# Batch 0's state softmax from scores with tokens as rows, and a new order for the first sixth of the steps

## The chip, the core and the metric

The kernel runs on one core of a Trainium2 chip. The metric is the device time of one execution, in microseconds, as the median of the runs.

## What is computed

```python
scores = scale * np.matmul(x, state.transpose(0, 1, 3, 2))     # x [8,8,512,64], state [8,8,32,64]
a = softmax over the 32 states (exp of scores minus their maximum, over sum + 1e-9)
xread = np.matmul(a, state)                                    # 512 rows per batch and head
scores2 = scale * np.matmul(state, x.transpose(0, 1, 3, 2))
a2 = softmax over the 512 tokens
sread = np.matmul(a2, x)                                       # 32 rows per batch and head
x = concat([xread, sread], axis=2), heads side by side: [4352, 512]
h = x @ w_in                                                   # w_in [512, 2048]
g = softplus(h)
out = g @ w_out                                                # w_out [2048, 512]
```

The weights of the MLP come as 64-bit numbers and are put together as fp32 on the chip.

## The kernel before

The eight heads of a batch go in two groups by the parity of the head (e = 0, 1); four heads of 32 states fill the 128 rows of a tile. For the token rows the first GEMM is not made from xread: the states times W ("V", `v_product`) are made first and then multiplied with the softmax weights (`gemm1`). TensorE makes the scores with states as rows and tokens as columns (`scores`, step Q); both softmaxes start from the same scores. The softmax over the tokens (steps e, f, i, t, u, R) runs along a row. The softmax over the states runs across rows: `a_turn` (step 1) turns blocks of 32 by 32 on VectorE so that the states of a token lie beside each other, `a_max`, `a_sub`, `a_exp`, `a_sum`, `a_mul` (2 to 6) work on groups of 32, and `a_back` (7) turns the result back on VectorE. For batch 0 the steps 1 to 7 go by halves of 256 tokens (two keys, (0, 0) and (0, 1)), both head groups in one tile; `span` gives the half. For the other batches a key is a head group.

W is loaded in ten pieces (step I) and each is put together in three steps: `win_upper` (a, ScalarE), `win_lower` (b, ScalarE or VectorE), `win_join` (c, VectorE). W_out (O) goes the same way by A, B, C and is then split into two fp32r parts, `wout_hi` (D) and `wout_lo` (E). Batch 0 goes through GEMM 1 (g), softplus (s) and GEMM 2 (G) directly; its first four column blocks of GEMM 1 and first two of GEMM 2 are full fp32, the rest three fp32r passes. The other batches use sums of blocks and products of their own (steps F, H, L, M and others), which the change does not touch.

The order is fixed: a string, `PLAN`, has one character for each step, and the kernel emits the steps in that order; each engine runs its own instructions in program order. SyncE issues all DMAs. A second table, `ENG`, names for some steps the engine that each occurrence runs on (D VectorE, A ScalarE, P GpSimd). Tiles live in "rooms": `take` gives out the tag that has been free longest, `done` counts down its uses. There are eight PSUM banks (`banks`).

```python
    for k in PLAN:
        now[0] = k
        count[k] = count.get(k, 0) + 1
        next(run[k])
```

All instructions are recorded with the line of one helper (L100), so the rows below are told apart by tile and shape: W, ST (the states), ident (transposes on TensorE), d, s, g, v (rooms in SBUF), b (PSUM banks).

Of the kernel before, what the change touches and what calls it, by code (L numbers as in the profile page):

```python
# [15 lines left out]
ALU = mybir.AluOpType  # L16
AX = mybir.AxisListType
PSUM = bass.MemoryType.PSUM

P = 128  # L20
B, H, S, NS, D = 8, 8, 512, 32, 64
# [8 lines left out]
F1, F2 = 4, 2  # L30
# [7 lines left out]
FORMS = (1, 2, 6, 5, 7, 3, 4)  # L38
SLAB = {5: 0, 6: 1, 7: 2, 4: 3, 1: 4, 2: 5, 3: 6}
PLAN = (  # L40
    "TSTSIITITIQI1IQ2O3e12e34dfbaafb4c565OOIIOc6vttQvahb7huecabfuhhbac78gtvggghe1cbhgguaA8c98BC89gvgshsGhll99DUGssB"
    "Am1EWCDbEn2fAaBmcnCgGggGGGGGgbABasmssDCcnEm3XjIXOOIKjvRGGnDsam4mAhhliAlBnBbcnCrYCbEGGggGgGGgGsaDDs2c3mmssEnjSj"
    "jjjjSjKjjjOjTTjOJvvGhhhll5m4hUnEGGgGgn5llU66WAsmdBmsGQvGnYChDlhnE7l7ei89eGggGGsWmsBA8Y9nmn1CUGgGGgKjjjKjKTKTjj"
    "jDffssmEWnY21U32gGGGtttWsouuuoQvvh1lefUYWhUGgshoggKjKKpjKJJjKXglUelogggssWsfsss4Fh3lYHWYggggKXKgsssssHHF5FLYLL"
    "MgRyMMKKppKJJpJJsFFzHkHLFH2LFLrZHkHH4HMMML5L66LkLkk7i1kHMJXXJJMRvvykr8Fh73q9l2h8H9qlkhh4HlMMJPXJJTJlzZkkk35Lgg"
    "gggsLkssss4vvMMgh5qkhlkHhdhsqLLqlllgMgggggMsssssFq67HkLJJJPJPPPXggggMssssHF8LHsHFM6LF7FHFLLkkHMMJJJPJHHkkqqkLL"
    "q98MMtytvuhzHkkuLHlFFLZLhvRMMJJPJJMMHl9kHkhHLHhkLgMMlkirqkLqLklkkPTJJPPJJPJJXXvQvgse1fhshhlq1ell2qh3qggggsssfs"
    "4ggMgggsH2l53LgMg4ssssssgggssHs5Fk6ki7LFHFFHLFHFLtytMMMMkLH6uzkuLZqkHvvRJJJJPTMMhhLlHH7hlHh8q98FLLllkkrMMJJJTJ"
    "XPLFqHLqkk9HLMMgggMMsHsskkqkkkLkJPPJJPTJJXPvQv1khhql2qlee13ggggssshsHfhf42llLgggMgggsHFqL35sss4ssgggMsssH56F6k"
    "LFHkLFH7MMttyF8HqFLu7L9kuzHkLFMJPJPJJMMMJJPPJPPRvHZkkHFqLiLkHh8vMMkLlrHhHhHqLlLlkkH9LLqMJXPTJPPJJJJMgMggMssshk"  # L50
    "kHkklkkvvQge1hfsgggshsshH2Lll3h1l2leLFgggg4sssfsggggssssgMMM3FHFqsH4F5FqqLH5Lqk6LTPPJJJPMtytMMJJXJHFFHkLiuk7kH"
    "HHHzL6HLqLZkukLMMkFMvvRJJPh8hH7kLqlq9LrqLh8MMMJTJPXJJJPPXJPl9kHkhkkklgMMskklkvQvgghqHl1ehe2sfhfLlh13lqgggssss4"
    "Lq253qgggwiMyPssgHs45MgJzlsgFPLstkuJgkxsgssgtgsMH6sqL7H86PuMFZRLvvkrFJkhlvhlPvhhFFJHFLhlh97MHLlHHMHLMwFkMkHJJ8"
    "hLJJJlPq9MHgLkxsgkgMFsslPwgHgLJqPkLghkMqMgxkHsskgPkskgLJgJgsllqsPLMHLHyzMqZsPwssMkgggqLggskg&P&wsxsxMgkqwkx%%s"
    "wgswx&xqP&%s%s&g%w&wP%wJsxxgwJxxw&x%&%sF&gFw&wx%&%qxg%wHx&s&Lg%H%&sL%&&%s%sHLHLMFHMHFPFJFHHkJFLFLFLLFJkHMLMFJk"
    "JHLHFkkJMHHLHkLqMHkPLHkFLLJLJHMHLqLJHFkMHPFqkLJLHHkHPFLHMMLJkLMHLHkkkkLJMLqMkPkkHHqPqkqLkqLqPPqMPMkPqMPkqkPP"
)
ENG = {
    '&': "DDAADDADDDDADADA",
    '3': "PPDDDPPDPDDPDDDP",  # L60
    '6': "PPDPPPPDDPDDDPPP",
    '8': "PPDPAPDPDPPDAADPDD",
    '9': "DPDPDDDPPDPDDPDDPP",
    'B': "DAAADDAA",
    'D': "PDPAAADA",
    'E': "DDDPDPPD",
    'F': "DPDDDDDDPDPDPDDPDDPDPDDPDDPDPPDPPDPDPDDDPDPPDPPDDPDDDDPDDDDDDPDD",
    'H': "PAAAAPAAAADPAADAPAAAAAAPADPPAAPDDPPDAAPAADDAPDAADADDPAADAAAPAPAPAAPADAAAPAPAAAAPADADAADAAAAAAAAPAAAAPAAADAAAAPAA",
    'L': "DDDDDDDDPDPDPPPDDDDPPDDDPDPPPDPDDDPDDPPPPPDDPDDDPDDPDPDDDPDDDPDDDPDDDDPDPDPDDPPDPPPPPPDDDDDDDDDDPDPDPDDDPDDDDPDD",
    'U': "PPDDDPDP",  # L70
    'W': "AAADAPAD",
    'Y': "DDDPPPDD",
    'b': "AAAAADDDDD",
    'h': "AAAADADDDDDDDADAADADDDAADDAAADADAADDAADADAAAADAAAAADADADADADDAAAAAAA",
    'k': "AADDDDDDDDDDDDDDAADDDDDDDDDDDDDDAADDDDDDDDDDDDDDAADDDDDDDDDDDDDDDDDDDDDDDDDDDDDDAADDDDDDDDDDDDDDAADDDDDDDDDDDDDDDDDDDDDD",
    'm': "DAADAADAAAPADP",
    'n': "DDDPDDDPPDPDDD",
    'o': "AAAD",
    'q': "PPDPDPDDPDPDDPDPPPDDDDPPPPPPPDDPDDPPDDDPPPDDPDDDDPPPDPDPDDDD",
    'u': "DAADDAADDADADDDD",  # L80
    'w': "PADDADAAAAAAAAAA",
    'x': "DDPPPPDPDDDDDPDP",
    'z': "DDADAADA",
# [51 lines left out]
def attention_then_softplus_mlp(ctx: ExitStack, tc, xn, xt, zq, zp, stk, w_in, w_out, out):  # L135
    nc = Ordered(tc) if PIN else tc.nc
# [13 lines left out]
    r2 = Rooms(sp, "s", N2, [P, 512])  # L150
    r4 = Rooms(sp, "d", N4, [P, 2, 512])
    banks = Rooms(ps, "b", 8, [P, 512])
    r1 = Rooms(sp, "v", N1, [P, P])
# [4 lines left out]
    ident = cp.tile([P, P], F32, name="ident")  # L158
    make_identity(tc.nc, ident)
    ST = cp.tile([P, B, 4, 2 * NS], F32, name="ST")  # L160
# [6 lines left out]
    def engine():  # L167

        k = now[0]
        i = count[k] - 1  # L170
        return ENG[k][i]

    def cast(dst, src, e):
        if e == "A":
            nc.scalar.copy(dst, src)
        elif e == "D":
            nc.vector.tensor_copy(dst, src)
        else:
            nc.gpsimd.tensor_scalar(dst, src, 1.0, 0.0, ALU.mult, ALU.add)

    def elementwise(dst, a, b, op, e):
        (nc.vector if e == "D" else nc.gpsimd).tensor_tensor(dst, a, b, op)
# [3 lines left out]
    xT, x, win, wraw = {}, {}, {}, {}  # L186
# [16 lines left out]
    def load_xT():  # L203
        for b, i in HALVES:
            if b == 0:
                t = xT[b, i] = r4.take([P, 4, S // 2])
                nc.sync.dma_start(t.t, xt[b, :, :, S // 2 * i:S // 2 * i + S // 2])
            else:
                t = xT[b, i] = r4.take()
                nc.sync.dma_start(t.t, xt[b, :, 2 * i:2 * i + 2, :])  # L210
            yield
# [123 lines left out]
    def units(b):  # L335
        return UNITS.get(b, UNIT)
# [3 lines left out]
    for b, f0, f1 in TURNS + [(b, 0, NFT) for b in range(2, B)]:  # L340
        for ft in range(f0, f1):
            i = next(i for i, (c0, c1) in enumerate(units(b)) if c0 <= P * ft < c1)
# [4 lines left out]
    def heads(out_e, b, rhs):  # L347
        for q in range(4):
            for e in range(2):
                r = slice(64 * e, 64 * e + 64)  # L350
                nc.tensor.matmul(out_e[e][32 * q:32 * q + 32], ST[r, b, q, 32 * e:32 * e + 32], rhs(q)[r], start=True, stop=True,
                                 tile_position=(64 * e, 32 * q))
# [37 lines left out]
    sc, T, e2, a2, pr, sr, aT = {}, {}, {}, {}, {}, {}, {}  # L390
# [6 lines left out]
    def span(b, u):  # L397
        return slice(S // 2 * u, S // 2 * u + S // 2) if b == 0 else slice(0, S)


    few = {}

    def mx(b, i):
        return few[b][:, 16 * i:16 * i + 16]
# [10 lines left out]
    def scores():  # L415
        for b in range(B):
            for u in range(2 if b == 0 else 1):
                n = S // 2 if b == 0 else S
                if u == 0:
                    sc[b, 0], sc[b, 1] = [banks.take(uses=4 if b == 0 else 3) for _ in range(2)]  # L420
                    few[b] = r1.take(uses=3)
                heads([sc[b, e][:, n * u:n * u + n] for e in range(2)], b, lambda q: xT[b, u][:, q] if b == 0 else xT[b, q // 2][:, q % 2])
                xT[b, u].done()
                if b:
                    xT[b, 1].done()
                yield

    def spread(t):
        return t.unsqueeze(2).broadcast_to([P, 16, NS])

    def flat(t):
        return t.rearrange("p a n -> p (a n)")

    def a_turn():
        for b, i in KEYS:
            t = T[b, i] = r2.take([P, 16, NS])
            if b == 0:
                for e in range(2):
                    nc.vector.transpose(flat(t[:, 8 * e:8 * e + 8]), sc[b, e][:, span(0, i)])
                    sc[b, e].done()  # L440
            else:
                nc.vector.transpose(flat(t.t), sc[b, i].t)
                sc[b, i].done()
            yield

    def a_max():
        for k in KEYS:
            nc.vector.tensor_reduce(mx(*k), T[k].t, AX.X, ALU.min if k[0] else ALU.max)
            yield

    def a_sub():
        for k in KEYS:
            elementwise(T[k].t, T[k].t, spread(mx(*k)), ALU.subtract, engine())
            yield

    def a_exp():
# [19 lines left out]
    af = {}  # L476

    def a_back():
        for k in KEYS:
            af[k] = r2.take(uses=4 + F1 if k[0] == 0 else 2)  # L480
            nc.vector.transpose(af[k].t, flat(T[k].t))
            T[k].done()
            yield

    def part(b, i, e):
# [462 lines left out]
    def fold_store():  # L948
# [13 lines left out]

    steps = {
        "S": load_state, "d": scale_state, "T": load_xT, "X": load_x, "I": load_win, "O": load_wout,
        "a": win_upper, "b": win_lower, "c": win_join,
        "A": wout_upper, "B": wout_lower, "C": wout_join, "D": wout_hi, "E": wout_lo,
        "v": v_product, "h": v_hi, "l": v_lo,
        "Q": scores, "1": a_turn, "2": a_max, "3": a_sub, "4": a_exp, "5": a_sum, "6": a_mul, "7": a_back,
        "8": a_hi, "9": a_lo, "e": s_max, "f": s_exp, "i": s_sum, "t": s_turn, "u": s_copy, "R": s_read,
        "r": s_scale, "y": s_back, "z": s_hi, "Z": s_lo,  # L970
        "w": w_hi, "x": w_lo, "g": gemm1, "&": h_copy, "%": h_add, "s": softplus, "m": g_hi, "n": g_lo, "G": gemm2,
# [67 lines left out]
```

## Time and profile before

| what | value |
|---|---|
| time, median of 3 runs | 615.14 us (614.76 to 615.14) |
| profiled execution, time | 614.1 us |
| its span | 612.3 us |
| TensorE matmul busy | 597.5 us (98%), 4048 passes |
| weight loads busy | 485.0 us |
| VectorE busy | 477.1 us (78%) |
| ScalarE busy | 306.9 us (50%) |
| GpSimd busy | 303.9 us (50%) |
| DMA | 161.62 MB, mean 264 GB/s |

The span is the part of the execution that the trace covers; 1.8 us of the profiled execution lie outside it. A busy time is the sum of the instructions' durations without their overlap. Matmul rows are pipelined, with modelled ends: the distance from one start to the next tells more of their price than their duration. An fp32 matmul is recorded as two passes, a transpose as one.

### The profile page before, as it was taken

To read this page: it belongs to the slowest core of one execution; us is meant where nothing else is said; L and a number is where in the kernel's file an instruction comes from. 1 tells how busy PE (TensorE), PEld (TensorE's weight loads), DVE (VectorE), ACT (ScalarE), POOL (GpSimd) and SP (SyncE) were. 2 spreads that over 40 slices of the span, in tenths; PEclk is the share of its full clock that TensorE was granted. 3 is DMA by queue.
4 is the path that set the end of the run, shared out by engine and by line. 5 is a ranking of instruction groups with operands and counts; after the bars stand their busy time and mean duration, and the time that the engine had idled before them with its cause. 6 is when DMAs were issued, how large, how long until landed. Compare 5 with 4: busy or idle time off the path is not lost.

```text
span 612.3 us, 10423 instructions
## 1 busy us (share of the span) xinstructions
PE 597.5 (98%) x4048; PEld 485.0 (79%) x4048; DVE 477.1 (78%) x644; ACT 306.9 (50%) x445; POOL 303.9 (50%) x190
## 2 busy tenths in 40 slices
PE   3999999999999999999999999999999999999997
PEld 1568677888788888878788787888787888888886
DVE  4999998799636896798479966699747944389996
ACT  4999767962526218631283318802675232274321
POOL 2422637517563761777276532672085955251561
PEclk9999999999999999999999999999999999999999
DMA  8999959999637888089917992699543851166572
GB/s 310 408 391 364 351 198 343 365 403 414 247 140 276 310 324 336 1 318 394 341 65 258 344 316 123 208 390 411 206 152 147 337 203 70 29 243 233 210 300 77
DMA packets 50415, 161.62 MB, mean 264 GB/s; under 512 B 4288, under 2 KB 29376, under 8 KB 37824
## 3 DMA queue, kind: packets, MB, share of 16 engines
q1 hardware_dynamic: 50368, 160.97, 70.5%
q8 instruction: 32, 0.52, 0.3%
q14 instruction: 15, 0.12, 0.1%
HBM read 137.36 MB, written 23.59 MB: 263 GB/s over the span
## 4 chain that ended last, share of the span: by engine, by line
PE 97%; DVE 1%; ACT 1%; DMA 1%; issue 0%; POOL 0%; SPq 0%
PE b L100 97%; ACT s L100 1%; DMA ST<-in_zp_dram 1%; DVE v L100 0%; DVE s L100 0%; POOL s L100 0%; SPq L100 0%; DVE W L100 0%; ACT ST L100 0%
## 5 line engine op out<-in xcount | busy, mean ns | idle before, releaser
L100 PE MATMUL b<-g,d 128*128 128x256 f32 (+1 forms) x1576 | 290.3, 337 | 0.0
L100 PEld LDWEIGHTS b<-g,d 128*128 128x128 f32 x1576 | 246.6, 190 | 36.1 <-issue 1.7
L100 PE MATMUL b<-d,d 128*128 128x512 f32 x744 | 177.2, 392 | 0.0
L100 PEld LDWEIGHTS b<-d,d 128*128 128x128 f32 x744 | 137.8, 188 | 32.3 <-issue 3.0
L100 ACT ACTIVATE g<-b 128x512 f32<-128x512 f32 x112 | 63.6, 600 | 98.7 <-PE b L100 98.3
L100 POOL TENSOR_TENSOR d<-g,d 128x1024 fp32r<-128x1024 f32 x31 | 78.6, 2538 | 53.0 <-ACT d L100 26.6
L100 DVE TENSOR_TENSOR s<-s,b 128x512 f32<-128x512 f32 (+1 forms) x105 | 68.7, 675 | 40.3 <-PE b L100 32.6
L100 DVE TENSOR_TENSOR d<-g,d 128x1024 fp32r<-128x1024 f32 x53 | 80.0, 1516 | 1.7 <-ACT d L100 1.5
L100 PE MATMUL b<-g,s 128*128 128x512 f32 (+1 forms) x280 | 71.4, 372 | 0.0
L100 ACT CAST d<-g 128x1024 fp32r<-128x1024 f32 x50 | 51.7, 1051 | 29.7 <-POOL g L100 15.8
L100 ACT ACT_TABLE_LOAD x48 | 61.6, 1283 | 1.5 <-PEq L1020 0.7
L100 PEld LDWEIGHTS b<-g,s 128*128 128x128 f32 x280 | 50.2, 188 | 12.0 <-issue 2.2
L100 ACT CAST d<-b 128x512 fp32r<-128x512 f32 x35 | 20.1, 586 | 59.3 <-PE b L100 59.3
L100 DVE TENSOR_TENSOR d<-b,d 128x512 fp32r<-128x512 f32 x62 | 41.4, 681 | 9.3 <-ACT d L100 9.0
L100 POOL TENSOR_SCALAR d<-g 128x1024 fp32r<-128x1024 f32 x20 | 29.5, 1476 | 36.2 <-DVE g L100 26.5
L100 POOL TENSOR_TENSOR s<-s,v 128x512 f32<-128x512 f32 x17 | 21.0, 1237 | 44.5 <-DVE v L100 43.9
L100 POOL TENSOR_TENSOR s<-s 128x256 f32<-128x256 f32 x29 | 29.9, 1032 | 21.1 <-DVE s L100 21.1
L100 POOL TENSOR_TENSOR d<-d,d 128x256 f32<-128x256 f32 (+2 forms) x17 | 28.3, 1664 | 18.6 <-DVE d L100 8.5
L100 PE MATMUL b<-W,ST 64*32 64x512 f32 (+2 forms) x544 | 32.6, 574 | 4.1 <-DVE W L100 4.1
L100 DVE TENSOR_REDUCE v<-s 128x16 f32<-128x512 f32 x32 | 21.6, 680 | 18.6 <-ACT s L100 18.5
L100 POOL TENSOR_TENSOR g<-g,g 128x1024 f32<-128x1024 f32 x11 | 29.4, 2671 | 11.2 <-DVE d L100 6.3
L100 ACT COPY s<-b 128x512 f32<-128x512 f32 (+2 forms) x32 | 15.2, 501 | 29.1 <-PE b L100 25.1
(82 smaller groups left out, 626.9 us busy)
## 6 DMA issues: line engine op xcount, KB each, us to landing
g<-slabs SPq DMA_DIRECT2D x98, 1024.0 KB, 6.6
d<-in_xt_dram SPq DMA_DIRECT2D x16, 512.0 KB, 7.4
g<-in_w_out_dram SPq DMA_DIRECT2D x8, 1024.0 KB, 12.5
d<-in_xn_dram SPq DMA_DIRECT2D x16, 512.0 KB, 7.6
slabs<-d SPq DMA_DIRECT2D x16, 512.0 KB, 6.9
out_dram<-s SPq DMA_DIRECT2D x56, 128.0 KB, 5.3
g<-in_w_in_dram SPq DMA_DIRECT2D x6, 1024.0 KB, 13.0
slabs<-g SPq DMA_DIRECT2D x24, 256.0 KB, 7.1
```

Source lines behind the costliest of these rows:

```text
L100: return lambda *a, **k: self.tc.keep_in_program_order(f(*a, **k))
```

## The change

Batch 0's softmax over the states no longer starts from the shared scores. `a_turn` has TensorE multiply again, with 128 tokens of x as weights and 64 state columns streaming, so that tokens come out as rows, into a PSUM bank of their own (`turned`). `a_max` and `a_sub` read that bank, both on VectorE; `a_sub` writes the SBUF tile. `a_back` is four transposes on TensorE into a bank (`back`) for each half, and a new step 0, `a_copy`, brings that bank to SBUF on ScalarE. The score banks of batch 0 have two uses instead of four, and its x tiles two instead of one. The other batches keep VectorE's transposes.

The first 278 of the 1758 characters of `PLAN` are replaced by 280: the same steps, each as often as before, and the two new ones, in another order. The engine entries of the occurrences in this stretch change too (those of 3, 6, 8, 9, B, D, E, U, b, h, m, n, u).

```diff
-    "TSTSIITITIQI1IQ2O3e12e34dfbaafb4c565OOIIOc6vttQvahb7huecabfuhhbac78gtvggghe1cbhgguaA8c98BC89gvgshsGhll99DUGssB"
...
+    "TSTSIITTQ1a2db1b3QI23ecfeac45f4vba56thIQvh6701Itc7haIbgc8he0auvggh1bufbgh8OggaAO9Osg8geIscXsBIcs9CvtGmh89f9DUl"
...
+    '0': "AA",
...
-    'D': "PDPAAADA",
...
+    'D': "DPAPDADA",
...
-                t = xT[b, i] = r4.take([P, 4, S // 2])
+                t = xT[b, i] = r4.take([P, 4, S // 2], uses=2)
...
-                    sc[b, 0], sc[b, 1] = [banks.take(uses=4 if b == 0 else 3) for _ in range(2)]
-                    few[b] = r1.take(uses=3)
+                    sc[b, 0], sc[b, 1] = [banks.take(uses=2 if b == 0 else 3) for _ in range(2)]
+                    few[b] = few.get(b) or r1.take(uses=3)
...
+    turned, back = {}, {}
+
     def a_turn():
         for b, i in KEYS:
-            t = T[b, i] = r2.take([P, 16, NS])
             if b == 0:
-                for e in range(2):
-                    nc.vector.transpose(flat(t[:, 8 * e:8 * e + 8]), sc[b, e][:, span(0, i)])
-                    sc[b, e].done()
+                few[b] = few.get(b) or r1.take(uses=3)
+                t = turned[i] = banks.take(uses=2)
+                for j in range(2):
+                    for q in range(4):
+                        nc.tensor.matmul(t[:, 256 * j:256 * j + 256].rearrange("p (e q n) -> p q e n", e=2, q=4)[:, q],
+                                         xT[b, i][:, q, P * j:P * j + P], ST[:, 0, q].rearrange("p (e n) -> p e n", e=2),
+                                         start=True, stop=True)
+                xT[b, i].done()
             else:
+                t = T[b, i] = r2.take([P, 16, NS])
                 nc.vector.transpose(flat(t.t), sc[b, i].t)
                 sc[b, i].done()
             yield
...
     def a_max():
         for k in KEYS:
-            nc.vector.tensor_reduce(mx(*k), T[k].t, AX.X, ALU.min if k[0] else ALU.max)
+            nc.vector.tensor_reduce(mx(*k), T[k].t if k[0] else grouped(turned[k[1]].t), AX.X, ALU.min if k[0] else ALU.max)
+            if k[0] == 0:
+                turned[k[1]].done()
             yield
...
     def a_sub():
         for k in KEYS:
-            elementwise(T[k].t, T[k].t, spread(mx(*k)), ALU.subtract, engine())
+            if k[0] == 0:
+                T[k] = r2.take([P, 16, NS])
+                nc.vector.tensor_tensor(T[k].t, grouped(turned[k[1]].t), spread(mx(*k)), ALU.subtract)
+                turned[k[1]].done()
+            else:
+                elementwise(T[k].t, T[k].t, spread(mx(*k)), ALU.subtract, engine())
             yield
...
     def a_back():
         for k in KEYS:
-            af[k] = r2.take(uses=4 + F1 if k[0] == 0 else 2)
-            nc.vector.transpose(af[k].t, flat(T[k].t))
+            if k[0] == 0:
+                t = back[k[1]] = banks.take()
+                for e in range(2):
+                    for j in range(2):
+                        nc.tensor.transpose(t[:, 256 * e + P * j:256 * e + P * j + P], flat(T[k].t)[:, 256 * j + P * e:256 * j + P * e + P], ident)
+            else:
+                af[k] = r2.take(uses=2)
+                nc.vector.transpose(af[k].t, flat(T[k].t))
             T[k].done()
+            yield
+
+    def a_copy():
+        for i in range(2):
+            af[0, i] = r2.take(uses=4 + F1)
+            cast(af[0, i].t, back[i].t, engine())
+            back[i].done()
             yield
```

## Rows read from the trace of the kernel before

**Rows 1.** Busy time and count of each engine by stretch, granted clock, DMA share.
```profile
0.00:18.40 18.40, 7.40 (x93) 3.53 (x93) 10.50 (x23) 9.86 (x21) 5.89 (x12) 1.00 0.89 326
18.40:130.00 111.60, 111.60 (x728) 83.71 (x728) 102.84 (x138) 91.31 (x120) 48.70 (x35) 1.00 0.97 347
...
600.00:612.30 12.30, 8.51 (x57) 7.60 (x55) 7.09 (x14) 0.69 (x1) 0.86 (x1) 1.00 0.27 85
```

**Rows 2.** TensorE's groups by form, 50 to 60 us: count, busy us, mean ns.
```profile
L100 PE MATMUL b<-g,s 128*128 128x512 f32 x28 | 6.8, 389 | 0.0
L100 PE MATMUL b<-d,d 128*128 128x512 f32 x18 | 4.4, 389 | 0.0
```

**Rows 3.** Timeline of TensorE in the opening: start, duration, what, wait before it.
```profile
5.10 1.11 PE L100 MATMUL b<-d,ST 64*32 64x256 f32 x16 [5.10 <-DMA ST<-in_zp_dram]
7.28 1.11 PE L100 MATMUL b<-d,ST 64*32 64x256 f32 x16 [1.07 <-DMA d<-in_xt_dram]
12.49 0.68 PE L100 MATMUL b<-W,ST 64*32 64x128 f32 x16 [4.10 <-DVE W L100]
13.10 1.97 PE L100 MATMUL b<-ident,s 128*128 128x128 f32 x8
15.00 1.39 PE L100 MATMUL b<-d,ST 64*32 64x512 f32 x16
...
18.40 0.66 PE L100 MATMUL b<-ident,s 128*128 128x128 f32 x4 [0.73 <-ACT s L100]
18.98 0.66 PE L100 MATMUL b<-W,ST 64*32 64x256 f32 x16
```

**Rows 4.** Timeline of TensorE at single transposes of the opening.
```profile
13.37 0.64 PE L100 MATMUL b<-ident,s 128*128 128x128 f32 x2
...
13.58 0.63 PE L100 MATMUL b<-ident,s 128*128 128x128 f32 x2
```

**Rows 5.** TensorE's groups by form, whole span.
```profile
L100 PE MATMUL b<-g,d 128*128 128x256 f32 x800 | 111.9, 282 | 0.0
...
L100 PE MATMUL b<-d,s 128*32 128x64 f32 x512 | 8.8, 221 | 0.0
```

**Rows 6.** Timeline of VectorE in the opening.
```profile
14.02 0.69 DVE L100 TENSOR_REDUCE v<-s 128x16 f32<-128x512 f32 x1 [0.49 <-ACT s L100]
14.74 0.17 DVE L100 TENSOR_SCALAR v<-v 128x16 f32<-128x16 f32 x1
14.95 0.25 DVE L100 RECIPROCAL v<-v 128x16 f32<-128x16 f32 x1
15.12 0.63 DVE L100 SCALAR_TENSOR_TENSOR W<-s,s 128x512 int32<-128x512 int32 x1
```

**Rows 7.** Timeline of ScalarE in the opening.
```profile
9.81 0.69 ACT L100 ACTIVATE s<-b,v 128x512 f32<-128x512 f32 x1
...
13.37 0.62 ACT L100 ACTIVATE s<-s 128x512 f32<-128x512 f32 x1
13.88 0.67 ACT L100 ACTIVATE s<-d 128x512 f32<-128x512 f32 x1
14.46 0.25 ACT L100 COPY s<-b 128x128 f32<-128x128 f32 x1
```

**Rows 8.** Timeline of GpSimd: a multiplication of the softmax, and two casts of W_out.
```profile
7.87 1.05 POOL L100 TENSOR_TENSOR s<-s,v 128x512 f32<-128x512 f32 x1 [6.56 <-DVE v L100]
...
27.00 1.05 POOL L100 TENSOR_SCALAR g<-d 128x1024 fp32r<-128x1024 f32 x1 [5.77 <-DVE d L100]
...
40.06 3.64 POOL L100 TENSOR_SCALAR g<-d 128x1024 fp32r<-128x1024 f32 x1 [8.95 <-ACT d L100]
```

**Rows 9.** SyncE's queue: the issue of W's first two pieces.
```profile
3.37 0.98 SPq L100 DMA_DIRECT2D d<-in_w_in_dram  x2
```

**Rows 10.** DMA issues of 3.8 to 4.3 us: count, KB each, us from issue to landing.
```profile
d<-in_w_in_dram SPq DMA_DIRECT2D x1, 512.0 KB, 6.7
```

More of the change, by code (lines that the diff above doesn't have):

```diff
@@ L40 @@
 PLAN = (
-    "TSTSIITITIQI1IQ2O3e12e34dfbaafb4c565OOIIOc6vttQvahb7huecabfuhhbac78gtvggghe1cbhgguaA8c98BC89gvgshsGhll99DUGssB"
[L42 to L55, printed above, removed]
@@ L56 @@
-    "JHLHFkkJMHHLHkLqMHkPLHkFLLJLJHMHLqLJHFkMHPFqkLJLHHkHPFLHMMLJkLMHLHkkkkLJMLqMkPkkHHqPqkqLkqLqPPqMPMkPqMPkqkPP"
+    "TSTSIITTQ1a2db1b3QI23ecfeac45f4vba56thIQvh6701Itc7haIbgc8he0auvggh1bufbgh8OggaAO9Osg8geIscXsBIcs9CvtGmh89f9DUl"
+    "GOhmAlBX2ECGOAbInaDEgGgnaBgCGGbccGAGusmsmBnODgWCEjsavnhYIAm3RlGjDjhjnTlbGsGgBciEmBjGsS4nAmgGCbKGG2asD3CESrGmcD"
+    "gsKgOdmsEnjvhl4hvB5n5lGGA6jghjjTU6sGlnhWgGslGUQmmjYjnjvJGjjOChDlhnE7l7ei89eGggGGsWmsBA8Y9nmn1CUGgGGgKjjjKjKTKT"
+    "jjjDffssmEWnY21U32gGGGtttWsouuuoQvvh1lefUYWhUGgshoggKjKKpjKJJjKXglUelogggssWsfsss4Fh3lYHWYggggKXKgsssssHHF5FLY"
@@ new lines @@
+    "LLMgRyMMKKppKJJpJJsFFzHkHLFH2LFLrZHkHH4HMMML5L66LkLkk7i1kHMJXXJJMRvvykr8Fh73q9l2h8H9qlkhh4HlMMJPXJJTJlzZkkk35L"
+    "gggggsLkssss4vvMMgh5qkhlkHhdhsqLLqlllgMgggggMsssssFq67HkLJJJPJPPPXggggMssssHF8LHsHFM6LF7FHFLLkkHMMJJJPJHHkkqqk"
+    "LLq98MMtytvuhzHkkuLHlFFLZLhvRMMJJPJJMMHl9kHkhHLHhkLgMMlkirqkLqLklkkPTJJPPJJPJJXXvQvgse1fhshhlq1ell2qh3qggggsss"
+    "fs4ggMgggsH2l53LgMg4ssssssgggssHs5Fk6ki7LFHFFHLFHFLtytMMMMkLH6uzkuLZqkHvvRJJJJPTMMhhLlHH7hlHh8q98FLLllkkrMMJJJ"
+    "TJXPLFqHLqkk9HLMMgggMMsHsskkqkkkLkJPPJJPTJJXPvQv1khhql2qlee13ggggssshsHfhf42llLgggMgggsHFqL35sss4ssgggMsssH56F"
@@ new lines @@
+    "6kLFHkLFH7MMttyF8HqFLu7L9kuzHkLFMJPJPJJMMMJJPPJPPRvHZkkHFqLiLkHh8vMMkLlrHhHhHqLlLlkkH9LLqMJXPTJPPJJJJMgMggMsss"
+    "hkkHkklkkvvQge1hfsgggshsshH2Lll3h1l2leLFgggg4sssfsggggssssgMMM3FHFqsH4F5FqqLH5Lqk6LTPPJJJPMtytMMJJXJHFFHkLiuk7"
+    "kHHHHzL6HLqLZkukLMMkFMvvRJJPh8hH7kLqlq9LrqLh8MMMJTJPXJJJPPXJPl9kHkhkkklgMMskklkvQvgghqHl1ehe2sfhfLlh13lqgggsss"
+    "s4Lq253qgggwiMyPssgHs45MgJzlsgFPLstkuJgkxsgssgtgsMH6sqL7H86PuMFZRLvvkrFJkhlvhlPvhhFFJHFLhlh97MHLlHHMHLMwFkMkHJ"
+    "J8hLJJJlPq9MHgLkxsgkgMFsslPwgHgLJqPkLghkMqMgxkHsskgPkskgLJgJgsllqsPLMHLHyzMqZsPwssMkgggqLggskg&P&wsxsxMgkqwkx%"
@@ L57 @@
+    "%swgswx&xqP&%s%s&g%w&wP%wJsxxgwJxxw&x%&%sF&gFw&wx%&%qxg%wHx&s&Lg%H%&sL%&&%s%sHLHLMFHMHFPFJFHHkJFLFLFLLFJkHMLMF"
+    "JkJHLHFkkJMHHLHkLqMHkPLHkFLLJLJHMHLqLJHFkMHPFqkLJLHHkHPFLHMMLJkLMHLHkkkkLJMLqMkPkkHHqPqkqLkqLqPPqMPMkPqMPkqkPP"
 )
@@ L59 @@
     '&': "DDAADDADDDDADADA",
[L60 to L64, printed above, removed]
-    'D': "PDPAAADA",
-    'E': "DDDPDPPD",
+    '0': "AA",
+    '3': "DDPDDPPDPDDPDDDP",
+    '6': "PPDDPPPDDPDDDPPP",
+    '8': "APADAPDPDPPDAADPDD",
+    '9': "PPPDDDDPPDPDDPDDPP",
+    'B': "DADDAAAA",
+    'D': "DPAPDADA",
+    'E': "DDDDDDPD",
     'F': "DPDDDDDDPDPDPDDPDDPDPDDPDDPDPPDPPDPDPDDDPDPPDPPDDPDDDDPDDDDDDPDD",
@@ L69 @@
     'L': "DDDDDDDDPDPDPPPDDDDPPDDDPDPPPDPDDDPDDPPPPPDDPDDDPDDPDPDDDPDDDPDDDPDDDDPDPDPDDPPDPPPPPPDDDDDDDDDDPDPDPDDDPDDDDPDD",
-    'U': "PPDDDPDP",
+    'U': "DPPDDPDP",
     'W': "AAADAPAD",
     'Y': "DDDPPPDD",
-    'b': "AAAAADDDDD",
-    'h': "AAAADADDDDDDDADAADADDDAADDAAADADAADDAADADAAAADAAAAADADADADADDAAAAAAA",
+    'b': "AAADAAAADA",
+    'h': "AAADDDADDADADADAADADDDAADDAAADADAADDAADADAAAADAAAAADADADADADDAAAAAAA",
     'k': "AADDDDDDDDDDDDDDAADDDDDDDDDDDDDDAADDDDDDDDDDDDDDAADDDDDDDDDDDDDDDDDDDDDDDDDDDDDDAADDDDDDDDDDDDDDAADDDDDDDDDDDDDDDDDDDDDD",
-    'm': "DAADAADAAAPADP",
-    'n': "DDDPDDDPPDPDDD",
+    'm': "PAPDPDDPPAAADP",
+    'n': "PDDDDPDPDDPDDD",
     'o': "AAAD",
     'q': "PPDPDPDDPDPDDPDPPPDDDDPPPPPPPDDPDDPPDDDPPPDDPDDDDPPPDPDPDDDD",
-    'u': "DAADDAADDADADDDD",
+    'u': "DDDDDAADDADADDDD",
     'w': "PADDADAAAAAAAAAA",
@@ L444, in a_turn, with grouped @@
             yield
+    def grouped(t):
+        return t.rearrange("p (a n) -> p a n", n=NS)
     def a_max():
         for k in KEYS:
-            nc.vector.tensor_reduce(mx(*k), T[k].t, AX.X, ALU.min if k[0] else ALU.max)
+            nc.vector.tensor_reduce(mx(*k), T[k].t if k[0] else grouped(turned[k[1]].t), AX.X, ALU.min if k[0] else ALU.max)
+            if k[0] == 0:
+                turned[k[1]].done()
             yield
@@ L967, in attention_then_softplus_mlp @@
         "v": v_product, "h": v_hi, "l": v_lo,
-        "Q": scores, "1": a_turn, "2": a_max, "3": a_sub, "4": a_exp, "5": a_sum, "6": a_mul, "7": a_back,
+        "Q": scores, "1": a_turn, "2": a_max, "3": a_sub, "4": a_exp, "5": a_sum, "6": a_mul, "7": a_back, "0": a_copy,
         "8": a_hi, "9": a_lo, "e": s_max, "f": s_exp, "i": s_sum, "t": s_turn, "u": s_copy, "R": s_read,
```

## The prediction

> **What bounds the kernel now.** I read the busy time by stretch first. TensorE is busy through all of 18.4 to 130 us; of the 14.8 us that its 597.5 fall short of the span, 11.0 lie before 18.4 us and 3.8 after 600 us [rows 1]. Then I asked whether a busy TensorE is also a quick one. In 50 to 60 us, 46 passes of 512 columns start in 10.0 us, which is 0.217 us each [rows 2]. Adding up all passes of 18.4 to 130 us at the paces seen there (some 371 of these at 0.217, the true fp32 ones at 0.44, the packed groups at 1.1) gives about 112 us for a stretch of 111.6, so no hidden wait is left there to win. The end of the kernel is therefore the moment at which TensorE gets going without a break, plus a fixed amount of work. That moment is 18.40 us, and the TensorE timeline of the opening shows how it comes about: waits of 5.10, 1.07, 4.10 and 0.73 us, the longest inside the opening being the one for the first joined piece of W at 12.49 [rows 3].
>
> As a marker I take the start of the third V product (W columns 256 to 512), at 18.98 us [rows 3]. By then TensorE has done both score steps of batch 0, two V products, the transposes of the token softmax (s_turn) for both head groups of batch 0 and the first head group of batch 1, the scores of batch 1 and one step of GEMM 1. After it, both orders have the same work left, but for what I add below.
>
> **What the change does to the opening.** Removed from VectorE: four 256-column transposes and two of 512. Their 3 us save nothing, since TensorE, not VectorE, sets the end from 18.4 us on. Added to TensorE: 16 matmuls with 128 token columns as weights and 64 state columns streaming, and eight 128x128 transposes. An fp32 matmul is two passes in the trace and a transpose is one (eight matmuls of a score step are 16 rows, four transposes are four [rows 3]), so that is 32 passes and 8 passes.
>
> No row shows a 128x128 weight load followed by a 64-column fp32 pass. The nearest is the transpose: the same load, 128 columns. At 18.40 us four take 0.58 us up to the next start, 0.145 each [rows 3]. In the opening they are slower: consecutive starts at 13.37 and 13.58 us, 0.21 apart [rows 4]. The clock column says 1.00 of 2.4 GHz there too [rows 1], so I go by the rows: the same 16 passes of 256 columns take 1.11 us at 5.10 and 0.66 at 18.98 [rows 3], and the slow ones stand behind waits of several microseconds. Bounds from both sides: the 128x64 passes with 32-column loads start 0.017 apart, four of them sharing the array, so 0.069 for four [rows 5]; above, 0.237, the 13.10 to 15.00 us of eight transposes [rows 3]. As TensorE now has no such wait between 5.10 us and the second turn step, I take 0.21 for the first turn step and 0.145 for the second.
>
> The first score step starts at 5.10 as before. It holds TensorE for about 0.9 us (its 1.11 less the overlap of the last records), so the first turn step starts at 6.0, ends 16 x 0.21 = 3.4 later at 9.4, the second ends 16 x 0.145 = 2.3 later, and with 0.2 for the drain its scores can be read at t = 11.9 us. The second half's x has landed by 7.28 [rows 3], so it delays nothing.
>
> From t on, the new order is one chain through four engines, each in program order. The second score step (0.9) runs beside it. VectorE: maximum of the second half 0.70 (a step that needs a reduction of 512 starts 0.72 after it did, 14.02 to 14.74), subtraction 0.65 (taken like a reduction of that size), the maximum over tokens and its scaling 0.85: t + 2.2 [rows 6]. ScalarE: the exponential over tokens 0.69 and the read of its sum (to t + 2.9), win_upper of W piece 1 0.6, then the exponential over states 0.62: t + 4.1 [rows 7]. VectorE: sum, epsilon, reciprocal 1.18 (14.02 to 15.20) [rows 6]: t + 5.3. GpSimd: the multiplication 1.05 [rows 8]: t + 6.4. TensorE: the four transposes of a_back 0.66 [rows 3]: t + 7.1. ScalarE: the new copy 0.6, a small V copy 0.2, win_upper of piece 3 0.6 [rows 7]: t + 8.5. VectorE: join of piece 3 0.7 [rows 6], a V copy 0.25: t + 9.45, and the third V product starts. The second half comes back in time: its product is ready at t + 7.75, its transposes end at t + 8.4, the first GEMM 1 step at t + 9.3, just before.
>
> So the marker moves from 18.98 to 11.9 + 9.45 = 21.35, 2.37 later. One thing is still undone then that was done before: s_turn of batch 1's first head group, 0.58. Together **+2.95 us**.
>
> A check by TensorE's work alone: between t and t + 9.45 it has 0.6 + 0.3 + 0.6 + 1.1 + 0.3 (scores, V, s_turn, scores of batch 1, V), 0.6 + 0.6 + 0.6 (a_back, s_turn, a_back) and 0.9 (GEMM 1), 5.6 us, so it waits 3.85, most of it 1.9 ahead of the first V product (join of piece 0 now stands behind three VectorE steps that need t) and 1.1 ahead of the first a_back.
>
> The other edits cost nothing beside this. The second half of batch 1's x is fetched ahead of W piece 2, which shifts that piece by one transfer; ScalarE reaches it at t + 5.4 = 17.3 and read it at 13.88 before [rows 7], so it is there. PSUM: the bank of each new tile was freed by a reader that comes earlier in the chain, the tightest by 0.2 us. Later on, W pieces 4 and 5 are joined at t + 15.9 and TensorE comes for them at t + 16.15; the first softplus of batch 0 ends at t + 17.65, its GEMM 2 step comes at t + 17.8. Both just hold. Casts that change engine lie off TensorE's path as long as this holds.
>
> The Trainium skill, "TensorE: Matmul & The Clock Gate", section "LDWEIGHTS (loading the stationary operand)", prices a load at its columns divided by 1.2 GHz, 107 ns for 128. No run here shows such a pass alone; the 256-column passes with the same load start 0.140 apart [rows 5], the transposes 0.145. At 0.107 for all 32 passes t would be 9.6 and the sum +0.65, no measurable change: the second rival below in another dress.
>
> **The rivals.** *First: TensorE's own work decides (faster).* If the dependent steps after t were shorter than their rows, TensorE would not wait between the second turn step and the marker. With 0.145 for all 32 passes t is 10.85, and 10.85 + 5.6 + 0.58 - 18.98 = -1.95, so 613.2 us. It decides faster only where the 3.85 us of waits shrink under 0.7. Each link has a row of its own shape, so I give it 0.08.
>
> *Second: the turn passes are cheap (no change).* If loads hide behind the pass before, 0.069 holds and t falls to 8.4. But then ScalarE is late: it must first make both halves of W pieces 0 and 1, and piece 1, the second of the two issued from 3.37 us on [rows 9], lands at 3.85 + 6.7 = 10.55 [rows 10]; another 0.6 and the token exponential starts at 11.15 instead of t + 2.2, the same as t = 8.95. Sum: 8.95 + 9.45 + 0.58 - 18.98 = 0.0, so 615.1, and up to 616.3 on the way there. For it: the later 64-column pace. Against: loads there are of 32 columns, and every pass with 128-column loads is at 0.14 or above. 0.17.
>
> *Third: one more wait downstream (slower still).* wout_hi of W_out rows 256 to 512 moves to GpSimd. By the rows it is needed (with wout_lo behind it) at t + 28.7 and, if GpSimd takes 1.05 us for it as at 27.00, ready at t + 28.4; at 3.64 as at 40.06 us [rows 8] it is t + 31.0 and TensorE waits 2.3: 620.4. The Trainium skill, "SBUF — State Buffer", section "SBUF: two separate sides", says that GpSimd and a VectorE operation with two SBUF inputs shut each other out; the long one did run beside joins with two inputs. Here VectorE's next instruction is the wout_lo that waits for this very cast, so it should be idle. 0.13.
>
> **How the numbers follow.** The profiled execution took 614.1 us around a span of 612.3, and the median of the runs is 615.14; the sum moves the one to 617.05 and the other to 618.1, and the median is what I forecast. Its own range is t from 10.85 (all passes at 0.145, +1.9) to 13.0 (all at 0.21, +4.05), a little wider for slips of half a microsecond in the chain: 616.5 to 619.5, chance 0.62. Within 0.2% (1.23 us) is what a measurement of this kernel cannot tell from no change. Slower: 0.62 + 0.13 = 0.75; same 0.17; faster 0.08. The range for 8 in 10 leaves out the first rival and the far end of the third: 614.9 to 620.8.
>
> **What would show it.** Right: the first turn step at about 6 us and the second ending near 11.7; a TensorE wait of nearly 2 us before the first V product near 14.8 and one of about 1 us before the first a_back near 18.3; the third V product at 21 to 22 us; no wait of TensorE from there to the last 10 us. Wrong if the turn passes start 0.1 us apart or less, if the third V product starts before 19.5, or if TensorE waits somewhere past 25 us.

## The result and the profile after

The changed kernel takes 619.19 us in the median (618.92 to 620.74, 6 runs) against 614.83 (614.4 to 615.14, 6 runs) for the kernel before: a ratio of 1.0077, 95% interval 1.0064 to 1.009. It is slower by 4.36 us by the medians, inside the range of the forecast; its own sum was 2.95. The two profiled executions lie 5.2 us apart (spans of 617.5 and 612.3), because that of before (614.1 us) was one of its quicker ones.

The opening on TensorE (timeline of the changed kernel; columns as in [rows 3]):

```profile
4.97 1.11 PE L101 MATMUL b<-d,ST 64*32 64x256 f32 x16 [4.97 <-DMA ST<-in_zp_dram]
6.00 7.09 PE L101 MATMUL b<-ST,d 128*128 128x64 f32 x32
13.02 1.11 PE L101 MATMUL b<-d,ST 64*32 64x256 f32 x16
15.99 0.68 PE L101 MATMUL b<-W,ST 64*32 64x128 f32 x16 [1.86 <-DVE W L101]
16.60 1.11 PE L101 MATMUL b<-ident,s 128*128 128x128 f32 x4
17.64 1.96 PE L101 MATMUL b<-d,ST 64*32 64x512 f32 x16
19.35 0.68 PE L101 MATMUL b<-W,ST 64*32 64x128 f32 x16
19.96 2.05 PE L101 MATMUL b<-ident,s 128*128 128x128 f32 x12
21.84 1.03 PE L101 MATMUL b<-s,s 128*128 128x256 f32 x4
22.80 1.33 PE L101 MATMUL b<-W,ST 64*32 64x256 f32 x16
24.06 6.31 PE L101 MATMUL b<-s,s 128*128 128x256 f32 x28
...
31.32 0.66 PE L101 MATMUL b<-ident,s 128*128 128x128 f32 x4
31.82 3.60 PE L101 MATMUL b<-d,s 128*128 128x512 f32 x8
```

The 32 turn passes run from 6.00 to 13.02 us: 0.219 us each, the second step no quicker than the first. The third V product, which started at 18.98 us and gave way at 19.58 before [rows 3], starts at 22.80 and gives way at 24.06: 4.48 us later. The s_turn that was done by then before comes at 31.32 and takes 0.50. One wait is new further down (list of TensorE's waits):

```profile
PE b L101 <- DMA g<-slabs: 0.4, 1, 0.4
```

The sum of 4.48, 0.50 and 0.36 (the wait for a slab at 135.87 us) is 5.34 against 5.2 between the spans. The change does not bring the wait for the slab each time: the runs below with the fourth V copy on ScalarE and with the joins early have the same turn steps and do not show it. Between the opening and the slab, TensorE is as full as before (windows, as in [rows 1]): 111.55 us busy with 727 passes in 111.6, where it had 728.

```profile
22.40:134.00 111.60, 111.55 (x727) 83.43 (x726) 101.52 (x137) 93.53 (x123) 48.28 (x37) 1.00 0.94 330
```

### The profile page after: what moved, and what is told of

Read it like the earlier page. It is cut to its first block, busy times and chain, and to the rows that moved or that the text cites. A ratio compares the mean times of both kernels' runs of the same rounds, so it can differ in the third digit from the quotient of the medians.

```text
span 617.5 us, 10501 instructions
## 1 busy us (share of the span) xinstructions
PE 606.5 (98%) x4088; PEld 493.0 (80%) x4088; DVE 476.1 (77%) x640; ACT 309.2 (50%) x446; POOL 300.4 (49%) x189
## 4 chain that ended last, share of the span: by engine, by line
PE 93%; DMA 3%; DVE 2%; POOL 1%; issue 0%; ACT 0%; SPq 0%; DVEq 0%; ACTq 0%
PE b L101 93%; DMA g<-slabs 2%; DMA slabs<-d 1%; POOL d L101 1%; DVE v L101 1%; DMA ST<-in_zp_dram 1%; DVE s L101 0%; DVE d L101 0%; DVE W L101 0%; ACT s L101 0%; SPq L101 0%; POOL s L101 0%; DVEq L101 0%; ACTq L101 0%
## 5 line engine op out<-in xcount | busy, mean ns | idle before, releaser
L101 ACT CAST d<-b 128x512 fp32r<-128x512 f32 x38 | 21.8, 586 | 60.5 <-PE b L101 60.5
L101 POOL TENSOR_TENSOR s<-s,v 128x512 f32<-128x512 f32 x15 | 19.6, 1310 | 51.5 <-DVE v L101 51.5
L101 DVE TENSOR_REDUCE v<-s 128x16 f32<-128x512 f32 x30 | 20.2, 678 | 18.1 <-ACT s L101 18.0
L101 DVE TENSOR_TENSOR d<-d,d 128x1024 fp32r<-128x1024 f32 (+2 forms) x25 | 29.3, 1173 | 1.2 <-POOL d L101 0.9
```

The costliest lines, as they stand in the source:

```text
L101: return lambda *a, **k: self.tc.keep_in_program_order(f(*a, **k))
```

## The experiments

Theory A: the loss is made in the opening, by the turn passes and the chain behind them, and the end moves with the moment at which TensorE gets going. The rivals: V, the new order costs something further down; U, 0.22 us is the price of such a pass at any pace. Each run stands beside runs of the kernel before on the same chip, with medians of 614.98 to 615.09.

**TensorE at work before the first score step.**

```diff
+    def warm():
+        while True:
+            t = banks.take()
+            for _ in range(8):
+                nc.tensor.matmul(t[:, 0:P], ident, ident, start=True, stop=True)
+            t.done()
+            yield
-    "TSTSIITTQ1a2db1b3QI23...
+    "TSTSIITT!Q1a2db1b3QI23...
```

> The changed kernel, with eight fp32 matmuls of the identity (16 passes, some 3.4 us) on TensorE ahead of the first score step, in the time in which it waits for the first x. Theory A (the 32 turn passes start 0.22 us apart because TensorE runs at its slow pace in the opening): with TensorE at work before 5 us the turn passes start about 0.145 us apart, the second turn step ends near 10.4 us instead of 13.1, and the kernel ends 2 to 3 us earlier: 616.5 against 619.2. Rival U (0.22 us is what a 128-column load with a 64-column fp32 pass costs at any pace): the turn passes stay at 0.22 and the time stays at 619.2. Between them: the passes start quick and fall back to 0.22 on the way, 617.5 to 618.5.

616.68 us, ratio 1.0027 (1.0015 to 1.0039). Its TensorE timeline:

```profile
1.35 3.78 PE L102 MATMUL b<-ident 128*128 128x128 f32 x16 [1.35 <-POOL ident masks.py:199]
...
6.06 3.79 PE L102 MATMUL b<-ST,d 128*128 128x64 f32 x32
9.77 0.66 PE L102 MATMUL b<-d,ST 64*32 64x256 f32 x16
12.73 0.68 PE L102 MATMUL b<-W,ST 64*32 64x128 f32 x16 [2.30 <-DVE W L102]
13.35 1.11 PE L102 MATMUL b<-ident,s 128*128 128x128 f32 x4
14.39 1.95 PE L102 MATMUL b<-d,ST 64*32 64x512 f32 x16
16.10 0.46 PE L102 MATMUL b<-W,ST 64*32 64x128 f32 x16
...
21.18 6.31 PE L102 MATMUL b<-s,s 128*128 128x256 f32 x28
```

The turn passes start (9.77 - 6.06) / 32 = 0.116 us apart, half of 0.219 and less than the 0.145 that I had for the quick pace. U is out: what TensorE did before sets the price. The third V product gives way at 21.18 instead of 24.06, 2.88 earlier; at the end 2.5 us of that arrive by the medians, 3.1 by the ratios and 1.9 between the spans of the two profiled executions. After the wait of 2.30 us the passes are slow again: four transposes in 1.04, the scores of batch 1 in 1.71. The granted clock tells why: this trace's clock records say 1.00 (2.4 GHz) from 5.96 to 12.78 us, then 0.50 (1.2 GHz) up to 16.20, and 1.00 from there to the end of the work (windows, as in [rows 1]; the last 0.50 is the clock).

```profile
13.50:16.00 2.50, 2.50 (x20) 1.00 (x28) 2.35 (x6) 2.50 (x7) 0.52 (x1) 0.50 1.06 401
```

In the changed kernel the same two steps take the same 1.04 and 1.71 us (16.60 to 17.64 to 19.35).

**Each turn matmul twice.**

```diff
-                for j in range(2):
+                for j in (0, 1, 0, 1):
```

> The changed kernel with each matmul of the two turn steps done twice, into the same place (32 passes more). Theory A (the end of the turn steps moves the end of the kernel one for one): 32 x 0.22 = 7.0 us later, 626.2; if the pace rises during the longer steps, 32 x 0.145 = 4.6, 623.8. Rival V (the turn steps lie beside other waits, and the loss comes from the order further down): under 2 us later, 619 to 621.

628.0 us, ratio 1.0206 (1.0191 to 1.0221).

```profile
5.96 13.92 PE L101 MATMUL b<-ST,d 128*128 128x64 f32 x64
19.80 1.11 PE L101 MATMUL b<-d,ST 64*32 64x256 f32 x16
```

64 passes take 13.84 us to the next start, 0.216 each; the pace does not rise in all that time. The steps end 6.78 us later than in the changed kernel and the kernel 8.8 later by the medians (7.9 by the ratios to the runs beside each). A's one for one is there, V's "under 2 us" is not. The third V product gives way 7.14 us later (31.20 against 24.06). So some more than one for one is lost, 1.1 us by the ratios and 2.0 by the medians, part of it behind the opening: a GEMM 2 step waits 0.40 us at 56.04. The sums of W_out's blocks on VectorE, beside GpSimd's work, take longer than in the changed kernel (1.20 and 1.84 us against 0.69 and 1.58); that they make this wait is not shown.

**The new path in the old order.** The changed code with `PLAN` and `ENG` of before and a step 0 behind each 7 of batch 0.

```diff
-    "...vttQvahb7huecabfuhhbac78gtvggggh...
+    "...vttQvahb70huecabfuhhbac708gtvggggh...
+    '0': "AA",
```

> The new path (scores with tokens as rows, transposes back on TensorE, the copy on ScalarE right after each) in the order and with the engines of the kernel before. Theory A (the path costs, in any order, as its passes stand ahead of everything that waits for TensorE): 618.5 to 620.5, near the changed kernel. Rival V (the new order costs): near the kernel before, 615 to 616.

622.39 us, ratio 1.0114 (1.0099 to 1.0129): worse than either theory said.

```profile
10.68 3.67 PE L101 MATMUL b<-ST,d 128*128 128x64 f32 x16
17.11 0.68 PE L101 MATMUL b<-W,ST 64*32 64x128 f32 x16 [2.77 <-DVE W L101]
23.82 0.63 PE L101 MATMUL b<-ident,s 128*128 128x128 f32 x4 [0.77 <-ACT s L101]
26.30 0.71 PE L101 MATMUL b<-W,ST 64*32 64x256 f32 x16
```

With all that stood ahead of it before, the third V product starts at 26.30 instead of 18.98 [rows 3], 7.32 later, and 7.3 is the loss by the medians. The turn passes hold TensorE until 14.3 us, and from there it waits for the chain (2.77, 0.77 and more). For this path the old order is the worse one, by 3.2 us by the medians and 2.3 by the ratios.

**The old path in the new order.** The code of before with the new `PLAN` and `ENG`, without step 0.

```diff
-    "TSTSIITTQ1a2db1b3QI23ecfeac45f4vba56thIQvh6701Itc7haIbgc8he0auvggh...
+    "TSTSIITTQ1a2dbb3Q1I23ecfeac45f4vba56thIQvh671Itc7haIbgc8heauvggh...
```

> The new order and engines with the old path: VectorE's transposes in the places of the turn and back steps, no copy; the second turn step stands behind the second score step, which it needs. Theory A: without the turn passes the token exponential starts near 11.4 us instead of 15.4, and the kernel ends within 1 us of the kernel before, 614 to 616. Rival V (the new order costs): 617.5 to 619.5.

618.15 us, ratio 1.0048 (1.0031 to 1.0066). My expectation missed. The token exponential started at 12.16 us, near the 11.4 I gave it, but the third V product then stopped half way (TensorE, then VectorE):

```profile
18.71 0.64 PE L101 MATMUL b<-W,ST 64*32 64x256 f32 x8
21.01 0.64 PE L101 MATMUL b<-W,ST 64*32 64x256 f32 x8 [1.66 <-DVE W L101]
```

```profile
18.49 0.70 DVE L101 STREAM_TRANSPOSE s<-s 128x512 f32<-128x512 f32 x1
19.11 0.70 DVE L101 TENSOR_SCALAR s<-d 128x512 int32<-128x512 int32 x1
19.92 1.03 DVE L101 SCALAR_TENSOR_TENSOR W<-s,s 128x512 int32<-128x512 int32 x1
```

It waits for the join of W piece 3, which stands on VectorE behind the transposes back and the lower part of that piece, an instruction that the new order brought to VectorE. So the order does cost with the old path, 3.06 us, and V's figure is right there: 1.99 us by the third V product (21.57 to 19.58), 0.5 for the late s_turn, 0.80 in a wait at 47.22. Path and order do not add up: 7.3 and 3.1 alone, 4.4 together.

The order has a share in the changed kernel's loss too, in the opening itself. The token exponential on ScalarE starts at 9.81 us in the kernel before [rows 7]; here, with the warm start, and in the changed kernel it starts at

```profile
12.16 0.69 ACT L101 ACTIVATE s<-b,v 128x512 f32<-128x512 f32 x1 [0.47 <-DVE v L101]
12.18 0.69 ACT L102 ACTIVATE s<-b,v 128x512 f32<-128x512 f32 x1 [0.63 <-DVE v L102]
15.43 0.69 ACT L101 ACTIVATE s<-b,v 128x512 f32<-128x512 f32 x1 [4.04 <-DVE v L101]
```

In the new order the state maxima and subtractions of both halves stand on VectorE ahead of the maximum that it waits for; before, that maximum came ahead of the second half's (8.47 against 10.07 us). Of the 5.6 us by which it is late in the changed kernel, 3.2 come with the slow turn passes, and 2.4 remain with quick ones, about as much as with the old path (whose first loads landed some 0.4 us later). From there to the end of the third V product the changed kernel takes 8.6 us, where the kernel before took 9.8.

**The fourth V copy on ScalarE.** `'h': "AAADDD...` becomes `"AAAADD...`.

> The changed kernel with the fourth copy of a V product (step h, fourth occurrence) on ScalarE instead of VectorE. In the changed kernel the second half of the third V product starts at 23.47 us, after that copy, which stands on VectorE behind the join of W piece 3 (22.52 to 23.2) and frees a PSUM bank. Theory A (the bank is a second wait, right behind the join's): the second half starts at 23.2, 0.2 to 0.3 us earlier, and the kernel ends as much earlier, 618.9, too little to be told apart by the median. Rival (the bank alone holds it): 22.95, 0.5 us earlier, 618.7. Rival (the copy on ScalarE delays ScalarE's later steps as much): no change in the trace from 40 us on.

619.54 us, ratio 1.0062 (1.0044 to 1.0081), which does not tell it from the changed kernel. In the trace the third V product runs without a stop from 23.50 and gives way at 24.09, where it was 24.06. That does not test the bank: TensorE itself came no sooner. The twelve transposes ahead take 2.45 us up to the next start (20.09 to 22.54) instead of 1.88, because they quicken from 0.213 to 0.109 us apart only at 22.4 us, and at 20.7 in the changed kernel. Whether the bank is a second wait stays open.

**The joins of pieces 0 and 1 ahead of the second maximum.**

```diff
-    "TSTSIITTQ1a2db1b3QI23ecfeac45f4v...
+    "TSTSIITTQ1a2db1b3accQI23efe45f4v...
```

> The changed kernel with the upper part of W piece 1 (ScalarE) and the joins of pieces 0 and 1 (VectorE) ahead of the second half's maximum, in the time in which ScalarE and VectorE wait for the second turn step. The wait of 1.9 us ahead of the first V product goes. Theory A (the chain from the second turn step through maxima, exponentials and the multiplication sets the opening; the joins cost only their own time in it, 0.6 on ScalarE): the wait comes back ahead of the transposes after it, the third V product starts 0.6 us earlier, 618.5. Rival W (the wait for the join is the loss of the opening): 1.9 us earlier, 617.3.

618.75 us, ratio 1.0049 (1.0034 to 1.0064).

```profile
13.87 0.68 PE L101 MATMUL b<-W,ST 64*32 64x128 f32 x16
16.53 1.09 PE L101 MATMUL b<-ident,s 128*128 128x128 f32 x4 [1.99 <-ACT s L101]
...
19.86 2.78 PE L101 MATMUL b<-ident,s 128*128 128x128 f32 x12
...
24.03 6.31 PE L101 MATMUL b<-s,s 128*128 128x256 f32 x28
```

The wait of 1.86 us ahead of the first V product is gone and 1.99 stand ahead of s_turn instead. That speaks against W and is what A said of the wait. But the 0.6 us of A do not come: the multiplication on GpSimd starts 0.47 earlier (18.27 against 18.74), yet a_back starts at 19.86 against 19.96, because TensorE itself, at the slow pace, is busy with scores and V until then, and its twelve transposes then take 2.62 us instead of 1.88, since the pace rises only at 22.5 us and not at 20.7. What the early joins would give at equal pace is not shown. The times do not decide either: 0.4 us quicker than the changed kernel by the medians, 1.7 by the ratios; the 0.5 between the two spans is the wait for the slab, which is absent here.

**All three together.**

> The changed kernel with all three: TensorE at work ahead of the first score step, joins early, the fourth V copy on ScalarE. Theory A for the opening: 2.7 + 0.6 + 0.3 us earlier by the third V product, near 20.5 us. Theory A2 (behind the opening the new order has a floor of its own, GEMM 2's inputs at about 45 us, as the runs with the warm start and with the old path in the new order showed): what comes earlier by the third V product is partly given back by a wait there, and the time ends at 616 to 616.7, no lower than the warm start alone. Rival (no such floor): 615.5 to 615.8.

618.25 us, ratio 1.0042 (1.0027 to 1.0057), later than either theory. The early joins stand on VectorE ahead of the maximum that is now ready sooner, and wait for ScalarE and W piece 1:

```profile
12.33 0.69 DVE L102 SCALAR_TENSOR_TENSOR W<-s,s 128x512 int32<-128x512 int32 x1 [0.52 <-ACT s L102]
12.94 0.68 DVE L102 TENSOR_REDUCE v<-b 128x16 f32<-128x512 f32 x1
```

TensorE waits 3.74 us for the token exponential, is slow again after it (granted clock 0.50 from 13.56 to 20.39 us), and the third V product gives way at 23.29. It says nothing on a floor further down: there TensorE shows no wait.

**The kernel before with TensorE at work.** The same eight matmuls ahead of the first score step and of the first V product (`"...TI!QI1..."` and `"...Oc6!vttQ..."`).

> The kernel before with eight fp32 matmuls of the identity ahead of the first score step and eight more ahead of the first V product, so that TensorE is at work through its waits. Theory A (the slow pace costs the opening wherever passes stand on the chain): the first V product, the transposes and the scores of batch 1 take about 1.0 us less, and the break-free stretch starts 0.4 to 1.0 us before 18.40: 614.0 to 614.6. Rival (the opening of the kernel before is set by ScalarE, VectorE and GpSimd, not by the pace of the passes): 615.0.

615.24 us, ratio 1.000 (0.999 to 1.0009).

```profile
12.52 0.45 PE L100 MATMUL b<-W,ST 64*32 64x128 f32 x16 [1.14 <-DVE W L100]
12.91 1.09 PE L100 MATMUL b<-ident,s 128*128 128x128 f32 x8
13.93 1.83 PE L100 MATMUL b<-d,ST 64*32 64x512 f32 x16
...
18.46 0.66 PE L100 MATMUL b<-ident,s 128*128 128x128 f32 x4 [0.79 <-ACT s L100]
```

The eight transposes take 1.02 us to the next start instead of 1.90 [rows 3], and s_turn of batch 1 still starts at 18.46 (18.40 before). In the kernel before, the pace of the opening costs nothing, as other engines set it. The rival is right.

**The changed kernel kept at work.** The warm start and six more matmuls of the identity ahead of the first V product (`"...f4!vba5..."`).

> The run with the warm start (eight matmuls of the identity ahead of the first score step), and six more ahead of the first V product, so that TensorE is at work in the 2.3 us in which it waits there. In the run with the warm start alone the passes after that wait were slow again (s_turn 1.04 us for four transposes, the scores of batch 1 1.71). Theory A (the pace of TensorE is what is left of the loss in the opening): those two take 0.6 and 1.1, and the third V product comes 0.5 to 1.0 us earlier, 615.8 to 616.2. Theory B (with the warm start the chain through VectorE, ScalarE and GpSimd sets the opening, and TensorE waits for the multiplications ahead of both a_back steps): s_turn and the scores are quicker, and the third V product ends at 21.2 us as before, 616.7.

617.92 us, ratio 1.0046 (1.0032 to 1.0059). In the profiled execution the first scores start at 5.81 instead of 5.06, since the first load of states landed later; I compare from the end of the turn steps on.

```profile
10.14 0.66 PE L102 MATMUL b<-d,ST 64*32 64x256 f32 x16
10.73 1.61 PE L102 MATMUL b<-ident 128*128 128x128 f32 x12
13.10 0.45 PE L102 MATMUL b<-W,ST 64*32 64x128 f32 x16 [0.76 <-DVE W L102]
13.48 0.66 PE L102 MATMUL b<-ident,s 128*128 128x128 f32 x4
14.07 1.09 PE L102 MATMUL b<-d,ST 64*32 64x512 f32 x16
14.95 0.63 PE L102 MATMUL b<-W,ST 64*32 64x128 f32 x16
16.97 1.09 PE L102 MATMUL b<-ident,s 128*128 128x128 f32 x8 [1.39 <-POOL s L102]
...
21.55 6.31 PE L102 MATMUL b<-s,s 128*128 128x256 f32 x28
```

All passes are quick now (the clock records say 1.00 from 5.73 us on), and TensorE waits 1.39 us for GpSimd's multiplication ahead of a_back. From the end of the turn steps to the end of the third V product it is 21.55 - 10.14 = 11.41 us, and 21.18 - 9.77 = 11.41 with the warm start alone. In the trace Theory B holds: once the turn steps are over, what is left is the chain through the four engines. Its time does not: 617.92 us is 1.2 more than it said. The late load accounts for 0.75 in the profiled execution; the rest stays open. No version here beats the kernel before.

## Why the prediction was right, and what was mis-sized

The place and the mechanism held: the third V product marked the loss, the turn passes and the chain behind them made it, and TensorE ran almost without a break from there on. What came is the case that gave the range its upper end, all 32 passes at the slow pace (t = 13.0, +4.05). That 615.14 + 4.05 is the measured median to the hundredth is luck: the chain behind t ran later than that sum has it, and the kernel before came out 0.3 us lower.

*The turn steps.* The first starts at 6.00 (6.0). The term that was off is the second step's pace: I took 0.145, and both ran at 0.219, so the scores could be read at 13.1 us instead of 11.9 (the maximum starts at 13.13). That is 1.2 of the missing microseconds. I had reasoned that TensorE, with no wait since 5.10 us, would quicken; it did not in 7.0 us of such passes, nor in 13.8. The prediction's clock of 1.00 for the opening was not a reading: in the kernel before, the trace's clock records begin at 15.68 us, and a stretch without one counts as 1.00 in that column. To go by the rows was the right choice.

*The chain.* Up to the multiplication the rows gave it well: the token exponential at t + 2.3 (t + 2.2), GpSimd's multiplication at t + 5.6 (t + 5.3). There a second slip of the same kind: I let TensorE wait 1.1 us for it. At the slow pace it was busy instead, a_back began at 19.96, t + 6.85, and its four transposes and the next engines' work ran late, so that the third V product began at t + 9.7 (t + 9.45) and was held at half way until 23.47, after the join of W piece 3 (22.52 to 23.21) and the VectorE copy that frees its bank (which of the two held it is not shown). In the sum it gave way 4.48 us later, where I had 2.37.

*What came free.* The wait ahead of the first V product was 1.86 us (1.9), and running the joins early only moved it.

*The rivals.* TensorE's own work did decide for a stretch, but by being slow, so the first rival pointed the wrong way. The second, cheap passes, is true of a TensorE that has been at work: 0.116. The Trainium skill, "TensorE: Matmul & The Clock Gate", section "LDWEIGHTS (loading the stationary operand)", prices a load at its columns divided by 1.2 GHz, an estimate of 0.107 us for 128; the trace is close to it at the quick pace and shows about twice that at the slow one (0.219). The third did not happen, by the very row named: the cast on GpSimd took 1.05 us with VectorE waiting for it (GpSimd, then VectorE).

```profile
39.43 1.05 POOL L101 TENSOR_SCALAR g<-d 128x1024 fp32r<-128x1024 f32 x1 [3.74 <-DVE d L101]
```

```profile
40.51 1.23 DVE L101 TENSOR_TENSOR g<-d,g 128x1024 fp32r<-128x1024 f32 x1 [1.17 <-POOL g L101]
```

*The signs.* The first turn step's start and the wait ahead of the first V product came as said. The second step ended at 13.0 us (11.7), TensorE did not wait ahead of the first a_back (about 1 us), and the third V product started at 22.80 (21 to 22). The wait for a slab of 0.36 us at 135.87 is by the letter one of the signs of being wrong, a wait past 25 us; I had not looked for it, and it is 0.36 of 5.2.

*What stays open.* The transpose of the first state read (s_back, after the stretch that the new order covers) starts at 125.0 us in the kernel before and at 129.1 in the run with the old path: 4.1 later, of which 1.99, 0.5 and 0.80 are placed above. In the doubled run it starts 8.4 us later than in the changed kernel (138.0 against 129.6), of which 7.14 and 0.40 are placed. The 0.8 and 0.9 left have no wait that the trace names. With the warm start 1.8 of the 2.88 us gained are left there (127.8); a wait of 0.30 us for VectorE at 45.88 is new, the rest is not placed.

## What to carry to other kernels

Work moved from an engine that is off the path to one that sets the end has to be priced at that engine's pace in that place, here 0.219 us a pass in the opening and not the 0.145 of a row taken in mid-flow. When a wait is taken away, ask which engine is late next: here the wait for the join, once removed, stood again one step on. And an order is made for one set of costs: the same order gains 2 to 3 us with one path and loses 3 with the other. Last, read the pace from records of one form: the clock column said 1.00 where there was no record of the clock.

## What the runs showed of the hardware

TensorE's pace followed what it had done before: 0.219 us for a turn pass that follows a start out of idleness, 0.116 for the same pass after 3.8 us of identity matmuls and the score step. In the changed kernel the clock column says 1.00 (2.4 GHz) throughout the opening, but the trace's first clock record begins at 20.72 us. The transposes that start at 19.96 are 0.213 us apart before that moment and 0.109 behind it. Where the records do cover a slow stretch, with the warm start, they say 0.50 (1.2 GHz), behind a wait of 2.30 us, and the same steps take the same time as in the changed kernel. So the slow pace of the opening is that of the lower clock: shown for the warm start, and for the changed kernel worked out from these equal times. The Trainium skill, "TensorE: Matmul & The Clock Gate", section "What's actually happening", says that the throttled clock, 1.2 GHz, is the default state and that activity releases it to 2.4 GHz; the rows agree, with 1.9 between the two paces of the turn passes. In the doubled run the pace was 0.216 us over all 13.8 us of turn passes, and the first clock record begins at 25.76 us.
